# Raw tokens of the next pair in tiles of products 4 and 6, parts made in the order of the products, loads issued by GpSimd

## The chip, the cores and the metric

The kernel runs on one core of one Trainium2 chip. The metric is the device time of one execution in microseconds (us); the figure is the median of the runs. PE is TensorE, DVE is VectorE, ACT is ScalarE, POOL is GpSimd. SP is SyncE, which only issues DMAs here.

## The reference

```python
# q, k, v: (8, 12, 448, 64) f32; w_pre, w_post: (12, 12)
scores = einsum('bhij,hg->bgij', scale * (q @ k^T), w_pre)
attn   = einsum('bhij,hg->bgij', softmax(scores), w_post) @ v
x      = attn as 3584 tokens x 768
h      = x @ w_in                  # 768 x 2048
out    = (h - tanh(h)) @ w_out     # 2048 x 768
```

The change touches only the second half, the feed-forward part from `x` to `out`, and only the way in which its input `x` is brought in.

## The kernel before, in words

The 3584 tokens make seven blocks of 512. Attention runs first, one pipeline of "places" `p` up to `NPL`, and writes `x` to DRAM (`xs`). Block 0 of the feed-forward part is done plainly (`Block0`, 16 steps). The other six blocks are done as three pairs (`s` = 0, 1, 2): a pair's tokens and each weight are split into halves, and the 2x2 matrix product is made with seven products instead of eight (Strassen-Winograd). So each pair needs seven inputs of the first layer, in this order: `b11`, `b21`, `t2`, `t1`, `t3`, `b22`, `t4` (table `WA`). The pair's tokens are four quarters b11, b21, b12, b22 (512 tokens x 384 channels, 768 KB each); three of them are inputs themselves, and the `t` are sums and differences of the four. Each input is held as a high part in fp32r (suffix `h`, a cast on ACT) and a low part (suffix `l`, a subtraction on DVE), since the matmuls are run as three products high x high, high x low, low x high. So there are 14 tiles, one buffer each, and one scratch tile `xr`.

A pair has eight steps (`pair_step`, `p` = 0 to 7). In a step the seven products of one slice of hidden channels run on PE, each 9 matmuls. After product `i`, `between(i)` is called, and then some units of the second layer (`res.units`), 12 matmuls each, which work on results stored earlier: an item of work has two units (four for block 0) and needs one activation tile `gl` (512 KB, loaded by SP, cast to `gh` on ACT, low part on DVE at L449) and a weight tile `w` (768 KB, loaded by SP). The weight tiles of the products are `wa` (384 KB, SP, seven buffers). `gl` and `w` have three buffers each, `gh` two, and they are loaded two items ahead.

Between two pairs lies a transition. PE runs held-back units (18 for s = 0 and s = 1) while DVE and ACT finish the last step (`Late`, v0 to v5) and make the 14 tiles of the next pair. `xq_jobs` is a generator of 11 jobs for that. In the first pair its jobs run within the steps of `Block0`. `xq_loads` is the generator of the loads of the four raw quarters, split by channel third and by sequence, six DMAs a quarter, issued by SP. Raw quarters go to `b11l`, `b21l`, `t3l` and `b22l`. In the last step of a pair (`p` = 7) `between(i)` issues them in small pieces. A load has to wait until the last product that reads its tile is done.

What sets the order: each engine executes its instructions in the order in which the code is written (`in_order` at the end). Each DMA on SP, and likewise each on POOL, signals one of eight semaphores in turn, so an issue waits until the eighth DMA before it on that queue has landed. POOL's own DMAs here are the stores of gate results (`gs<-ga`, `gs<-gb`, `gs<-gs`, from v0 and v5) and of outputs.

Of the kernel before, what the change touches and what calls it, by code (L numbers as in the profile page):

```python
# [21 lines left out]
def raw(ap):  # L22

    return ap.bitcast(F32)
# [126 lines left out]
def kernel_body(  # L151
# [11 lines left out]
    nc = tc.nc  # L163
# [92 lines left out]

    LATER = ("b21h", "b22h", "t4h")

# [300 lines left out]

    def load_xq(name, b, h):  # L560
        x_tiles(name)
        for c in range(HK):
            for to, i, at in runs(b):
                nc.sync.dma_start(raw(ff.xs[name])[:, c, to], xs[i][:, h * HK + c, at])
            yield

    def xq_jobs():

        def sub(x, y):
            nc.vector.tensor_sub(xr, x if x is xr else raw(ff.xs[x]), y if y is xr else raw(ff.xs[y]))  # L570

        def high(x, src):
            x_tiles(x + "h")
            nc.scalar.copy(ff.xs[x + "h"], src)

        def low(x, src):
            nc.vector.tensor_sub(ff.xs[x + "l"], src, raw(ff.xs[x + "h"]))

        def both(x):
            high(x, raw(ff.xs[x + "l"]))  # L580
            low(x, raw(ff.xs[x + "l"]))

        xr = ff.xr.tile([P, HK, TB], F32, name="xr", tag="xr")
        def parts(x):
            high(x, xr)
            low(x, xr)

        sub("t3l", "b11l")
        yield
        x_tiles("t1l")  # L590
        parts("t1")
        yield
        sub("b22l", "t3l")
        yield
        parts("t3")
        yield
        nc.vector.tensor_add(xr, xr, raw(ff.xs["b11l"]))
        yield
        both("b11")
        yield  # L600
        x_tiles("t2l")
        parts("t2")
        yield
        sub("b21l", xr)
        yield
        both("b21")
        yield
        both("b22")
        yield
        x_tiles("t4l")  # L610
        parts("t4")
        yield

    IDLE = ("u", "qa", "qb", "t", "h01", "h23")
    def xq_loads(s):
        ba, bb = 2 * s + 1, 2 * s + 2
        order = (("b11l", ba, 0), ("b21l", ba, 1), ("t3l", bb, 0), ("b22l", bb, 1))
        for x, b, h in order if s else (order[0], order[2], order[3], order[1]):
            yield from load_xq(x, b, h)

# [114 lines left out]
    with ExitStack() as st:  # L735
# [501 lines left out]
        def between0(f):  # L1237
            if f in (10, 12):
                res.more_w2((f - 10) // 2)
            if f in (13, 15):  # L1240
                res.more_gr((f - 13) // 2)
            for _ in range({1: 2, 2: 1, 4: 1, 5: 1, 6: 1, 8: 1, 10: 1, 12: 1, 14: 1}.get(f, 0)):
                next(xq)

        xq, xl = xq_jobs(), xq_loads(0)
        pieces = {NPL - 2: 2, NPL - 1: 3, NPL: 3, NPL + 1: 2, NPL + 2: 2}
        x0 = [partial(parts_x0, c, nc.vector if c < 4 else nc.gpsimd) for c in range(NK)]
# [73 lines left out]
    for s in range(NS):  # L1321
        for p in range(NQ):

            def between(i):
                next(xq, None)
                if p == NQ - 1 and s + 1 < NS:
                    for _ in range((2, 2, 2, 0, 1, 3, 2)[i]):
                        next(xl, None)

# [7 lines left out]
        else:  # L1337
            res.deepen()
        job = partial(next, xq, None)
        jobs = [  # L1340
            [late.v0], [late.v1, late.v2], [late.v3], [late.v4], [late.v5, job], [job, job], [job, job], [job, job], [job, job],
        ]
        n = HELD[s] + AHEAD[s]
        for i in range(0, n, 2):
            res.units(1)
            for f in jobs.pop(0) if jobs else ():
                f()
            for _ in range(2):
                next(xl, None)
            res.units(1)  # L1350
# [37 lines left out]
```

## Time and profile before

| | |
|---|---|
| median of 3 runs | 1745.02 us (1744.99 to 1750.26) |
| profiled execution | 1741.7 us, span of the core 1740.0 us |
| PE busy | 1673.0 us, 96% |
| DVE / ACT / POOL busy | 1232.8 / 1142.9 / 489.3 us |
| block 0 | about 856 to 927 us |
| steps of s = 0 | 927 to 1083 us; transition to about 1132 us |
| steps of s = 1 | to 1330 us; transition to about 1391 us |
| steps of s = 2 and the tail | to 1740 us |

A row of windows gives, for a stretch, its length and then the busy time of each engine, the granted PE clock (1.00 is full), the busy share of the DMA engines and GB/s. In a timeline the first number is the start, the second the duration, and the brackets give idle time ahead of the instruction and what ended it. "DMA" rows in the chain are transfers from issue to landing.

### The profile page before, as it was taken

The numbers are of one execution on the slowest core, as the hardware profiler recorded it, in microseconds if no ns is written. First come the engines' busy times: TensorE is split into PE (matmuls) and PEld (weight loads), VectorE is DVE, ScalarE is ACT, GpSimd is POOL, SyncE is SP. The second block draws the span as 40 slices with busy tenths as digits, with TensorE's granted clock in tenths as the row PEclk, the third lists the DMA queues.
The fourth block names the chain that finished last, engine by engine and source line by source line (L and its number), as shares of the span: only waits on it lengthen the run. The fifth ranks groups of instructions, "written<-read, shape, count | busy, mean of one in ns | idle before, by whom it ended". The sixth has DMA issues, their size and how long they took to land.

```text
span 1740.0 us, 41171 instructions
## 1 busy us (share of the span) xinstructions
PE 1673.0 (96%) x16068; PEld 1391.5 (80%) x16068; DVE 1232.8 (71%) x2119; ACT 1142.9 (66%) x2016; POOL 489.3 (28%) x702
## 2 busy tenths in 40 slices
PE   8999999999999899999998999899998899999999
PEld 6776777777777677777787778788887888889999
DVE  5686777766777777775498899668776768788432
ACT  5777777777778787786486767456665365666331
POOL 1355455555545555551100111101101101101000
PEclk9999999999999999999999999999999899999999
DMA  8778789787887979865778889879989779888993
GB/s 179 212 224 254 229 253 277 234 261 240 244 254 232 260 250 266 260 198 171 234 263 301 283 290 328 321 270 349 317 309 374 286 252 351 297 313 328 406 414 138
DMA packets 322289, 475.09 MB, mean 273 GB/s; under 512 B 105264, under 2 KB 255280, under 8 KB 322096
## 3 DMA queue, kind: packets, MB, share of 16 engines
q1 hardware_dynamic: 305660, 414.34, 73.9%
q0 software_dynamic: 16128, 57.68, 8.6%
q8 instruction: 128, 2.10, 0.5%
q14 instruction: 65, 0.53, 0.1%
q10 hardware_dynamic: 308, 0.43, 0.1%
HBM read 274.73 MB, written 120.59 MB: 227 GB/s over the span
## 4 chain that ended last, share of the span: by engine, by line
PE 76%; DVE 8%; DMA 6%; ACT 6%; issue 3%; SPq 1%; POOL 1%; DVEq 0%; ACTq 0%; POOLq 0%
PE ps_o L956 14%; PE ps_m L998 8%; PE ps_p L917 8%; PE y L533 6%; PE y L531 6%; PE y L532 6%; PE ps_h L290 6%; PE ps_h L291 6%; PE ps_h L293 6%; PE ps_q L873 6%; DMA vr<-in_v_dram 1%; PE ps_m L839 1%; DVE qa L319 1%; DMA t<-s 1%; DMA gl<-gs 1%
## 5 line engine op out<-in xcount | busy, mean ns | idle before, releaser
L956 PEld LDWEIGHTS ps_o<-wr,e 60*112 60x112 f32 (+1 forms) x5760 | 306.1, 175 | 45.2 <-POOL wr L939 12.2
L956 PE MATMUL ps_o<-wr,e 60*112 60x60 f32 (+1 forms) x5760 | 315.4, 259 | 17.2 <-ACT at L966 11.9
L926 DVE TENSOR_REDUCE mx<-ps_p 128x1 f32<-128x448 f32 x360 | 207.3, 618 | 154.3 <-PE ps_p L917 154.0
L928 ACT ACTIVATE e<-ps_p,mx 128x448 f32<-128x448 f32 x360 | 225.7, 634 | 104.2 <-DVE mx L926 93.4
L966 ACT COPY at<-ps_o 112x960 f32<-112x960 f32 x156 | 153.8, 986 | 76.9 <-PE ps_o L956 76.1
L939 POOL TENSOR_TENSOR wr<-wpost,zs 128x120 f32<-128x120 f32 x180 | 69.7, 387 | 422.8 <-DVE zs L938 319.1
L917 PE MATMUL ps_p<-t,wpre 60*64 60x448 f32 (+1 forms) x1440 | 180.9, 570 | 7.0 <-DMA t<-s 5.1
L998 PEld LDWEIGHTS ps_m<-at,vr 112*64 112x64 f32 x3072 | 147.5, 137 | 29.5 <-ACT at L973 11.5
L998 PE MATMUL ps_m<-at,vr 112*64 112x120 f32 (+1 forms) x3072 | 161.8, 261 | 6.8 <-ACT at L973 4.1
L531 PE MATMUL y<-w,gh 128*128 128x384 f32 x448 | 154.1, 344 | 5.7 <-ACT u L306 2.7
L533 PE MATMUL y<-w,gl 128*128 128x384 f32 x424 | 146.6, 346 | 8.1 <-DVE gl L449 8.1
L532 PE MATMUL y<-w,gh 128*128 128x384 f32 x448 | 153.1, 342 | 0.0
L873 PEld LDWEIGHTS ps_q<-kk,qh 64*120 64x120 f32 (+1 forms) x768 | 60.2, 177 | 85.3 <-issue 57.1
L873 PE MATMUL ps_q<-kk,qh 64*120 64x448 f32 (+1 forms) x768 | 124.6, 400 | 2.2 <-DVE kk L825 1.4
L878 DVE COPY s<-ps_q 120x448 f32<-120x448 f32 (+1 forms) x192 | 112.6, 615 | 9.9 <-PE ps_q L873 9.3
L306 ACT ACTIVATE u<-h 128x1024 f32<-128x1024 f32 x56 | 59.5, 1062 | 76.5 <-DVE h L715 71.4
L668 POOL DMA_DIRECT2D gs<-gb x24 | 17.2, 717 | 296.5 <-DVE gb L667 280.8
L878 ACT COPY s<-ps_q 120x448 f32<-120x448 f32 (+1 forms) x192 | 95.4, 539 | 7.0 <-PE ps_q L873 6.7
L443 ACT CAST gh<-gl 128x1024 fp32r<-128x1024 f32 x61 | 63.4, 1039 | 52.6 <-DMA gl<-gs 17.4
L531 PEld LDWEIGHTS y<-w,gh 128*128 128x128 f32 x448 | 86.6, 193 | 10.8 <-ACT u L306 3.0
L533 PEld LDWEIGHTS y<-w,gl 128*128 128x128 f32 x424 | 81.8, 193 | 9.6 <-DVE gl L449 9.5
L532 PEld LDWEIGHTS y<-w,gh 128*128 128x128 f32 x448 | 86.5, 193 | 3.4
(372 smaller groups left out, 3891.2 us busy)
## 6 DMA issues: line engine op xcount, KB each, us to landing
t<-s SPq DMA_DIRECT2D x342, 210.0 KB
wa<-ss SPq DMA_DIRECT2D x96, 384.0 KB
w<-wo SPq DMA_DIRECT2D x43, 768.0 KB
gl<-gs SPq DMA_DIRECT2D x62, 512.0 KB
wa<-wi SPq DMA_DIRECT2D x72, 384.0 KB
w<-ts SPq DMA_DIRECT2D x35, 768.0 KB
gs<-gs POOLq DMA_DIRECT2D x24, 768.0 KB, 9.3
cr<-in_moe_w_in_dram SPq DMA_DIRECT2D x48, 256.0 KB
```

Source lines behind the costliest of these rows:

```text
L290: nc.tensor.matmul(ph, w[:, c, 0], xh, start=start and c == 0, stop=False, skip_group_check=True)
L531: nc.tensor.matmul(y, gh[:, tok], wh, start=first, stop=False, skip_group_check=True)
L532: nc.tensor.matmul(y, gh[:, tok], wl, start=False, stop=False, skip_group_check=True)
L533: nc.tensor.matmul(y, gl[:, tok], wh, start=False, stop=last, skip_group_check=True)
L873: nc.tensor.matmul(ps[:n, :S], qx[a, hp, :], kx[a, hp % 2], start=(x == 0), stop=(x == 2))
L878: eng(sts[i][:n, 2 * hp + j, :], ps[:n, :S])
L917: nc.tensor.matmul(pss[r][halves[j], :], wpre[k, :], ts[j][k, :], start=True, stop=True)
L926: nc.vector.tensor_reduce(out=mx, in_=ps, axis=AX.X, op=ALU.max, negate=True)
L928: nc.scalar.activation(e, ps, AF.Exp, bias=mx, scale=1.0, accum_out=zs[:, 0, r : r + 1])
L956: nc.tensor.matmul(ps[:CP, j, c * GP : (c + 1) * GP].rearrange("p (h i) -> p h i", i=GI)[:, :, r * GH : (r + 1) * GH], e[k, c * CP : (c + ...
L966: nc.scalar.copy(ats[i0][:, :, :, at : at + 2 * GI].rearrange("p c h (j i) -> p j (c h) i", j=2), ps[:CP, :, : NC * GP].rearrange("p j (x ...
L998: nc.tensor.matmul(pv[j * D : (j + 1) * D, r, :n], vt[:, j, c, :], ats[i][:, c, 2 * hp + j, :n], start=(c == 0), stop=(c == NC - 1),)
```

## The change

The raw quarters go into other tiles: b11 into `t1l`, b21 into `b22h`, b12 into `t1h`, and b22 into `b22l`. These belong to products 3 and 5. A quarter is loaded with two DMAs (one per sequence) instead of six. For s = 0 SP issues them; for the two transitions POOL does, three in steps after products 4, 5 and 6, and the fourth after the first held unit. The 11 jobs are reordered to b11, b21, t3, t2, t4, t1, b22; each job keeps its instructions (seven casts on ACT, seven low parts and four sums on DVE). Eight jobs run in block 0 or in a transition and three (the difference for t1, t1's parts, b22's parts) in the next pair's first step, after products 0, 1 and 2; before it was 11 and 0 for the first pair and 9 and 2 for the others.

```diff
-    LATER = ("b21h", "b22h", "t4h")
+    LATER = ("t2h", "t4h", "t4l")
...
-    def load_xq(name, b, h):
+    def load_xq(eng, name, b, h):
         x_tiles(name)
-        for c in range(HK):
-            for to, i, at in runs(b):
-                nc.sync.dma_start(raw(ff.xs[name])[:, c, to], xs[i][:, h * HK + c, at])
-            yield
+        for to, i, at in runs(b):
+            eng.dma_start(raw(ff.xs[name])[:, :, to], xs[i][:, h * HK : (h + 1) * HK, at])
...
     def xq_loads(s):
         ba, bb = 2 * s + 1, 2 * s + 2
-        order = (("b11l", ba, 0), ("b21l", ba, 1), ("t3l", bb, 0), ("b22l", bb, 1))
-        for x, b, h in order if s else (order[0], order[2], order[3], order[1]):
-            yield from load_xq(x, b, h)
+        for x in (("t1l", ba, 0), ("b22h", ba, 1), ("b22l", bb, 1), ("t1h", bb, 0)) if s == 0 else (
+            ("t1l", ba, 0), ("t1h", bb, 0), ("b22h", ba, 1), ("b22l", bb, 1)
+        ):
+            load_xq(nc.gpsimd if s else nc.sync, *x)
+            yield
...
+        parts("b11", at("t1l"), "h", "l")
+        yield
+        parts("b21", at("b22h"), "h", "l")
+        yield
+        xr = fresh()
+        nc.vector.tensor_sub(xr, at("b22l"), at("t1h"))
+        yield
+        parts("t3", xr, "h", "l")
+        yield
+        nc.vector.tensor_add(xr, xr, at("t1l"))
+        yield
+        parts("t2", xr, "h", "l")
+        yield
+        nc.vector.tensor_sub(xr, at("b22h"), xr)
+        yield
+        parts("t4", xr, "h", "l")
+        yield
+        nc.vector.tensor_sub(xr, at("t1h"), at("t1l"))
+        yield
+        parts("t1", xr, "h", "l")
+        yield
+        parts("b22", at("b22l"), "h")
+        yield
...
-            for _ in range({1: 2, 2: 1, 4: 1, 5: 1, 6: 1, 8: 1, 10: 1, 12: 1, 14: 1}.get(f, 0)):
+            for _ in range({1: 1, 2: 1, 4: 1, 6: 1, 8: 1, 10: 1, 12: 1}.get(f, 0)):
                 next(xq)
...
-        pieces = {NPL - 2: 2, NPL - 1: 3, NPL: 3, NPL + 1: 2, NPL + 2: 2}
+        pieces = {NPL - 2: 1, NPL - 1: 1, NPL: 1, NPL + 1: 1}
...
                 next(xq, None)
-                if p == NQ - 1 and s + 1 < NS:
-                    for _ in range((2, 2, 2, 0, 1, 3, 2)[i]):
-                        next(xl, None)
+                if p == NQ - 1 and s + 1 < NS and i >= 4:
+                    next(xl, None)
...
-            [late.v0], [late.v1, late.v2], [late.v3], [late.v4], [late.v5, job], [job, job], [job, job], [job, job], [job, job],
+            [late.v0], [late.v1, late.v2], [late.v3], [late.v4, job], [late.v5, job], [job, job], [job, job], [job, job],
```

The first place is the end of the last step of s = 0. SP's queue there, before: the last of the 24 loads of raw tokens (`xs`), the one weight load of a product among them, and then the activation and weight tiles of the held units.

```order
L564 DMA b22l<-xs_61 128x192
L564 DMA b22l<-xs_62 128x320
L632 DMA wa<-ss_77 128x768
L564 DMA b22l<-xs_61 128x192
L564 DMA b22l<-xs_62 128x320
L564 DMA b22l<-xs_61 128x192
L564 DMA b22l<-xs_62 128x320
L376 DMA gl<-go 128x1024
L375 DMA w_15227<-wo_75 128x1536
L375 DMA w_15264<-wo_75 128x1536
L376 DMA gl<-go 128x1024
```

SP's queue at the same place in the changed kernel:

```order
L624 DMA wa<-ss_77 128x768 x3
L376 DMA gl<-go 128x1024
L375 DMA w_15195<-wo_75 128x1536
L375 DMA w_15235<-wo_75 128x1536
L376 DMA gl<-go 128x1024
L375 DMA w_15269<-wo_76 128x1536
L375 DMA w_15303<-wo_76 128x1536
L403 DMA gl<-gs_90 128x1024
```

All loads of `xs` have left SP's queue, and the tiles of the held units follow the weights of the products directly. POOL's queue in the same stretch, changed kernel (before, it held only the rows `gs` and `out_dram`):

```order
L660 DMA gs_90<-gb 128x2x512
L661 DMA gs_90<-gs 128x3x512
L563 DMA t1l<-xs_60 128x3x256
L563 DMA t1l<-xs_61 128x3x256
L563 DMA t1h<-xs_61 128x3x192
L563 DMA t1h<-xs_62 128x3x320
L563 DMA b22h<-xs_60 128x3x256
L563 DMA b22h<-xs_61 128x3x256
L638 DMA gs_90<-ga 128x2x512
L563 DMA b22l<-xs_61 128x3x192
L563 DMA b22l<-xs_62 128x3x320
```

Eight loads now stand behind the two stores of v5, and the store of v0 stands behind six of them.

The second place is the middle of the transition after s = 1, on DVE: `gl` is the low part for the next item of units, `c` adds results out of PSUM, the rest are jobs. Before:

```order
L570 TENSOR_TENSOR xr<-b22l,t3l 128x1536
L449 TENSOR_TENSOR gl<-gl,gh 128x1024
L577 TENSOR_TENSOR t3l<-xr,t3h 128x1536
L597 TENSOR_TENSOR xr<-xr,b11l 128x1536
L449 TENSOR_TENSOR gl<-gl,gh 128x1024
L550 TENSOR_TENSOR c<-y_17206,c 128x384
L550 TENSOR_TENSOR c<-y_17207,c 128x384
L550 TENSOR_TENSOR c<-y_17208,c 128x384
L550 TENSOR_TENSOR c<-y_17209,c 128x384
L577 TENSOR_TENSOR b11l<-b11l,b11h 128x1536
L577 TENSOR_TENSOR t2l<-xr,t2h 128x1536
L449 TENSOR_TENSOR gl<-gl,gh 128x1024
```

The same items in the changed kernel:

```order
L579 TENSOR_TENSOR t3l<-xr,t3h 128x1536
L449 TENSOR_TENSOR gl<-gl,gh 128x1024
L596 TENSOR_TENSOR xr<-xr,t1l 128x1536
L579 TENSOR_TENSOR t2l<-xr,t2h 128x1536
L449 TENSOR_TENSOR gl<-gl,gh 128x1024
L550 TENSOR_TENSOR c<-y_17162,c 128x384
L550 TENSOR_TENSOR c<-y_17163,c 128x384
L550 TENSOR_TENSOR c<-y_17164,c 128x384
L550 TENSOR_TENSOR c<-y_17165,c 128x384
L600 TENSOR_TENSOR xr<-b22h,xr 128x1536
L579 TENSOR_TENSOR t4l<-xr,t4h 128x1536
L449 TENSOR_TENSOR gl<-gl,gh 128x1024 x2
```

Behind the four `c` stood two low parts; now a difference and the low part made of it stand there, and no job stands between the last two `gl`.

The third place is the first step of s = 0, on DVE: the last gate of block 0 (`ga`), then the sum `h` that takes product 1 out of PSUM. Before:

```order
L326 TENSOR_TENSOR ga<-qa,u 128x1024
L329 COPY_PREDICATED ga<-gs,t 128x1024
L694 TENSOR_TENSOR h_13996<-ps_h,h_13996 128x512
L449 TENSOR_TENSOR gl<-gl,gh 128x1024
L715 TENSOR_TENSOR h_13996<-h_13996,ps_h 128x512
```

In the changed kernel:

```order
L326 TENSOR_TENSOR ga<-qa,u 128x1024
L329 COPY_PREDICATED ga<-gs,t 128x1024
L604 TENSOR_TENSOR xr<-t1h,t1l 128x1536
L686 TENSOR_TENSOR h_13975<-ps_h,h_13975 128x512
L579 TENSOR_TENSOR t1l<-xr,t1h 128x1536
L579 TENSOR_TENSOR b22l<-b22l,b22h 128x1536
L449 TENSOR_TENSOR gl<-gl,gh 128x1024
L707 TENSOR_TENSOR h_13975<-h_13975,ps_h 128x512
```

Three jobs have come in around `h`, and three fewer stand in block 0 ahead of these rows.

More of the change, by code (lines that the diff above doesn't have):

```diff
@@ L558, in x_tiles, with xq_loads @@
             ff.xs[x] = x_tile_of(x)
-    def load_xq(name, b, h):
+    def load_xq(eng, name, b, h):
         x_tiles(name)
-        for c in range(HK):
-            for to, i, at in runs(b):
-                nc.sync.dma_start(raw(ff.xs[name])[:, c, to], xs[i][:, h * HK + c, at])
+        for to, i, at in runs(b):
+            eng.dma_start(raw(ff.xs[name])[:, :, to], xs[i][:, h * HK : (h + 1) * HK, at])
+    def xq_loads(s):
+        ba, bb = 2 * s + 1, 2 * s + 2
+        for x in (("t1l", ba, 0), ("b22h", ba, 1), ("b22l", bb, 1), ("t1h", bb, 0)) if s == 0 else (
+            ("t1l", ba, 0), ("t1h", bb, 0), ("b22h", ba, 1), ("b22l", bb, 1)
+        ):
+            load_xq(nc.gpsimd if s else nc.sync, *x)
@@ L565, in load_xq @@
             yield
     def xq_jobs():
[L569 to L588, printed above, removed]
+        def parts(x, src, *tiles):
+            x_tiles(*[x + t for t in tiles])
+            hi, lo = ff.xs[x + "h"], ff.xs[x + "l"]
+            nc.scalar.copy(hi, src)
+            nc.vector.tensor_sub(lo, src, raw(hi))
+        def fresh():
+            return ff.xr.tile([P, HK, TB], F32, name="xr", tag="xr")
+        def at(x):
+            return raw(ff.xs[x])
+        parts("b11", at("t1l"), "h", "l")
@@ L589, in xq_jobs @@
         yield
-        x_tiles("t1l")
-        parts("t1")
+        parts("b21", at("b22h"), "h", "l")
         yield
-        sub("b22l", "t3l")
+        xr = fresh()
+        nc.vector.tensor_sub(xr, at("b22l"), at("t1h"))
         yield
-        parts("t3")
+        parts("t3", xr, "h", "l")
         yield
-        nc.vector.tensor_add(xr, xr, raw(ff.xs["b11l"]))
+        nc.vector.tensor_add(xr, xr, at("t1l"))
         yield
-        both("b11")
+        parts("t2", xr, "h", "l")
         yield
-        x_tiles("t2l")
@@ L602, in xq_jobs @@
-        parts("t2")
+        nc.vector.tensor_sub(xr, at("b22h"), xr)
         yield
-        sub("b21l", xr)
+        parts("t4", xr, "h", "l")
         yield
-        both("b21")
+        nc.vector.tensor_sub(xr, at("t1h"), at("t1l"))
         yield
-        both("b22")
+        parts("t1", xr, "h", "l")
         yield
-        x_tiles("t4l")
-        parts("t4")
+        parts("b22", at("b22l"), "h")
         yield
     IDLE = ("u", "qa", "qb", "t", "h01", "h23")
-    def xq_loads(s):
-        ba, bb = 2 * s + 1, 2 * s + 2
-        order = (("b11l", ba, 0), ("b21l", ba, 1), ("t3l", bb, 0), ("b22l", bb, 1))
-        for x, b, h in order if s else (order[0], order[2], order[3], order[1]):
-            yield from load_xq(x, b, h)
@@ L1347, in kernel_body @@
                 f()
-            for _ in range(2):
-                next(xl, None)
+            next(xl, None)
             res.units(1)
```

## The prediction

> **What bounds the kernel now.** The page says that PE is busy for nearly the whole span, so only stretches where PE stands still, or runs at a lower granted clock, can give time back.
>
> ```profile
> span 1740.0 us, 41171 instructions
> PE 1673.0 (96%) x16068; PEld 1391.5 (80%) x16068; DVE 1232.8 (71%) x2119; ACT 1142.9 (66%) x2016; POOL 489.3 (28%) x702
> ```
>
> Windows over the places that the change touches come next: the gates of block 0, its end with the first step of s = 0, the transition after s = 0, then the last step of s = 1 and the two halves of the transition behind it.
>
> ```profile
> 882.00:926.00 44.00, 44.00 (x195) 36.44 (x195) 42.23 (x34) 40.54 (x43) 3.25 (x6) 1.00 0.84 290
> 926.00:945.00 19.00, 14.42 (x63) 10.68 (x62) 15.79 (x14) 12.46 (x15) 1.21 (x3) 1.00 0.95 344
> 1083.00:1107.00 24.00, 18.68 (x98) 16.11 (x97) 17.89 (x16) 9.90 (x11) 2.18 (x3) 0.93 0.93 352
> 1300.00:1326.00 26.00, 26.00 (x129) 23.14 (x128) 20.06 (x19) 16.69 (x21) 1.80 (x3) 1.00 1.00 363
> 1326.00:1360.00 34.00, 28.37 (x133) 26.86 (x131) 21.94 (x22) 14.73 (x17) 6.56 (x11) 0.85 0.89 333
> 1360.00:1395.00 35.00, 28.85 (x139) 27.07 (x138) 24.31 (x21) 14.08 (x13) 3.63 (x6) 0.90 0.78 286
> ```
>
> In block 0 PE never waits (44.00 of 44.00), though DVE is 96% busy. PE then stands for 4.6 us up to 945. The first transition costs 5.3 us of idle time and 7% of clock, the second 5.6 + 6.2 us and 15% and 10% of clock. There are about 25 us to be had in all.
>
> Who PE waits for, in the first transition and then in the second:
>
> ```profile
> PE y L501 <- DMA w<-wo: 5.3, 1, 5.3
> PE y L531 <- ACT c L509: 1.4, 1, 1.4
> ...
> PE y L533 <- DVE gl L449: 8.1, 4, 2.8
> PE y L531 <- ACT u L306: 2.7, 1, 2.7
> PE y L531 <- DMA w<-ts: 1.0, 1, 1.0
> ```
>
> The chain of the first transition runs through the raw loads, and SP's own waits name why: its issues of raw tokens (L564) waited for PE to give a tile free and for earlier transfers to land.
>
> ```profile
> 1071.38 5.76 DMA b21l<-xs
> 1077.16 6.33 DMA w<-wo
> 1083.51 7.60 DMA t3l<-xs
> 1091.19 0.34 SPq L376
> 1091.57 7.00 DMA w<-wo
> 1098.70 0.77 PE y L501
> ...
> SPq L564 <- PE ps_h L291: 3.1, 1, 3.1
> SPq L564 <- DMA t3l<-xs: 2.2, 2, 1.6
> ...
> 1084.82 0.40 PE L501 MATMUL y<-w,gh 128*128 128x512 f32 x1
> ```
>
> So the weight tile that PE wanted at 1093.4 (5.3 ahead of 1098.7) was issued at 1091.57, since the small loads stood ahead of it. The last row is the first held unit: it starts a new item, which sets free the buffers for that issue, so the issue was some 6 us late.
>
> **The change, part by part.**
>
> *Raw loads off SP, first transition.* SP then issues `gl` and `w` at about 1085. A landing of 7.00 us as in the chain ends at 1092.3, ahead of 1093.4. The 5.3 us of waiting go, and with them the lowered clock behind it: 7% of 18.68 is 1.3. The wait on `c L509` (1.4) came from two casts that ACT ran between two groups of copies; now one cast stands there, so I take it as gone too. Against that, POOL's four quarters now move in the same 20 us in which the units load. Three weight tiles fall in that time, each with a lead of 8.3 us against landings of 7.0 to 9.1 (the last from a row below), so 0 to 0.8 late each: 0 to 2.4, and I take 1.5. Sum: -5.3 - 1.3 - 1.4 + 1.5 = -6.5.
>
> *The same in the second transition, first half.* The rows of two starts of items on PE, of SP's queue, of the cast and the matmul that waited, and the GB/s over 1326 to 1360 in 40 slices:
>
> ```profile
> 1326.25 0.33 PE L531 MATMUL y<-w,gh 128*128 128x384 f32 x1
> ...
> 1332.54 0.33 PE L531 MATMUL y<-w,gh 128*128 128x384 f32 x1
> ...
> 1327.98 0.81 SPq L403 DMA_DIRECT2D gl<-gs  x1
> ...
> 1332.10 4.04 SPq L564 DMA_DIRECT2D b22l<-xs  x4
> 1336.24 0.48 SPq L403 DMA_DIRECT2D gl<-gs  x1
> 1337.48 0.32 SPq L393 DMA_DIRECT2D w<-ts  x1
> 1337.55 1.04 ACT L443 CAST gh<-gl 128x1024 fp32r<-128x1024 f32 x1 [5.27 <-DMA gl<-gs]
> 1346.55 0.41 PE L531 MATMUL y<-w,gh 128*128 128x384 f32 x1 [1.00 <-DMA w<-ts]
> ...
> GB/s 410 347 396 395 381 370 357 323 355 396 424 433 420 409 281 267 409 401 396 425 448 412 405 414 417 400 416 406 399 336 101 0 0 0 81 207 207 316 372 401
> ```
>
> Items start on PE at 1326.3, 1332.5 and, without stalls, at 1336.7 and 1340.9; each start releases the buffers for the item two further on. The second pair of loads (1336.24 and 1337.48) was due at 1332.5, so SP was 4 to 5 us late with it. The landings took 9.5 us (1327.98 to 1337.5) and 9.1 (1337.48 to 1346.5). Issued on time and landing alike, the first pair arrives at 1336 (no stall) and the second at 1342.1, 1.2 after its item. Of this half's loss of 5.6 idle and 15% of 28.37 (4.3), together 9.9, that would leave 1.2.
>
> But the transfers themselves move later. Before, one quarter (0.79 MB) and, as I estimate, half of another were still to come at 1326. Now all four are, since on POOL they stand behind the stores of v5:
>
> ```profile
> 1326.78 0.75 POOL L669 DMA_DIRECT2D gs<-gs  x1
> ```
>
> That is 3.15 - 1.18 = 1.97 MB more in a stretch where the engines run full (28 slices, mean 390 GB/s): 5.0 us, if nothing of it finds a gap. The ends: 0 (the three empty slices, 2.6 us, and the thin ones behind them take it) and 6.1 (all of 2.36 MB). I take 5.0, since the DMA engines were at 1.00 already in 1300 to 1326 and SP's queue can't load further ahead than its buffers. So 9.9 becomes 6.2: -3.7.
>
> A rule speaks against this size. The Trainium skill, page "DMA: Bandwidth & Descriptors", section "SWDGE vs HWDGE vs iDMA", says that each DMA engine takes turns between the queue that GpSimd feeds and those that hardware feeds. By it SP's tiles would get half the rate as long as GpSimd's transfers last, and the sum would be that of the slower rival below, which is worked out there from rows; no row here has so long an overlap of the two queues.
>
> *Jobs in the second half.* Rows on ACT and DVE of the jobs between two `gl`:
>
> ```profile
> 1364.28 1.05 ACT L443 CAST gh<-gl 128x1024 fp32r<-128x1024 f32 x1 [3.11 <-DMA gl<-gs]
> 1365.24 1.47 ACT L574 CAST t1h<-xr 128x1536 fp32r<-128x1536 f32 x1
> ...
> 1366.74 1.76 DVE L577 TENSOR_TENSOR t1l<-xr,t1h 128x1536 fp32r<-128x1536 f32 x1 [2.60 <-ACT t1h L574]
> 1368.54 1.76 DVE L570 TENSOR_TENSOR xr<-b22l,t3l 128x1536 f32<-128x1536 f32 x1
> 1370.21 1.22 DVE L449 TENSOR_TENSOR gl<-gl,gh 128x1024 fp32r<-128x1024 f32 x1
> ...
> 1378.81 1.94 DVE L550 TENSOR_TENSOR c<-y,c 128x384 f32<-128x384 f32 x4
> ```
>
> `gh` starts, a cast (1.47) and two DVE operations (1.7 each) follow, then `gl` (1.2): 7.1 us, while an item lasts 4.2. That is why PE waits for `gl`. With the new order the sum comes before the cast and doesn't wait for it, so two of these chains shrink by 1.7 us. The third grows: behind the four `c` (1.9) come a difference (1.7), a cast that waits for it (1.5), its low part (1.8) and `gl`, 8.1 us, where 1.9 + 1.7 + 1.7 + 1.2 = 6.5 stood. The last chain sets when this half ends, so what the first two give the third takes back: 0, with -3.4 (both kept) and +1.6 as ends.
>
> *Three jobs moved to the next step.* In block 0 they took no time from PE (44.00 of 44.00), so only its end counts:
>
> ```profile
> 939.00 1.36 DVE L329 COPY_PREDICATED ga<-gs,t 128x1024 f32<-128x1024 int32 x1
> 940.22 0.71 DVE L694 TENSOR_TENSOR h<-ps_h,h 128x512 f32<-128x512 f32 x1
> ```
>
> Product 3 started behind that `h`, at 941.0. Two of the jobs that leave stood in the gate chain, 1.75 each, so the last gate ends 3.5 us earlier, at 936.7. Then t1's three pieces come in, and product 3 reads them: 1.7 + 1.5 + 1.8 in a row, with a little to hand over, until 941.7. So the gain is eaten: +0.6 (ends -1.1, if `h` alone counts, and +2). In the first step of s = 1, b22's parts stand ahead of a `gl`: the chain behind product 2 is 0.7 (an evacuation like that of `h`) + 1.5 + 1.8 + 1.2 = 5.2, and the matmul that needs it comes a unit, a product and two matmuls later, 2.1 + 2.1 + 0.4 = 4.6, so +0.6. In s = 2 no item begins there: 0.
>
> *At nothing.* The loads for block 0 (8 instead of 24 on SP, the same bytes): PE has no wait on them, and the reader of the last quarter comes in step 2; with that cover gone, a late quarter would hold DVE ahead of the gates. The waits that POOL gets: v0's store stands behind six loads there, and nobody reads it within the transition.
>
> **Sum:** -6.5 - 3.7 + 0 + 0.6 + 0.6 = -9.0 us. The profiled execution took 1741.7 us (1.7 of it around the span), which would be 1732.7. It lies 3.3 below the median of 1745.0, so the median goes to 1736.0.
>
> **The rivals.** *Transfers collide as before* (0.21). SP is free sooner, but the bytes meet on the same engines, the second transition gives 0, and half of the 5.3 stays in the first: -6.5 + 2.7 + 1.2 = -2.6, 1742.4. For it: DMA at 0.93 to 1.00 in all these rows. Against it: the empty slices around 1351, in which PE ran slow and SP had nothing free to issue. The Trainium skill, same page, section "Issuing engines are not separate DMA queues", holds that issuing from several engines saves only the issuing time; by that the time would be near this rival's. The rows agree that SP's time was the one on the chain.
>
> *Slower* (0.12): SP's tiles get only half of the rate. POOL moves 5.8 MB from 1326 on (three stores of 0.52, 0.79 and 0.52, outputs 0.79, quarters 3.15); at 195 GB/s that lasts 30 us. An item's 1.31 MB then take 6.7 us instead of 4.2, so the 4.4 items in that time lose 11.0, with the clock's 4.3 as now 15.3 in place of 9.9: +5.4. The first transition's item (2.1 MB) takes 10.8 instead of 8.4, three times: 7.2 in place of 8.0, -0.8. With the steps' +1.2 the sum is +5.8: 1750.8. It decides where `gl` takes over 10.5 us to land in 1326 to 1350.
>
> *More* (0.14): the second half also clears, as `gl` lands in 4.4 us. Its 6.2 idle and 10% of 28.85 go: -9 further, 1727.0.
>
> *The change doesn't do what it says*: `gl` and `w` are held by the wait for PE that the `wa` ahead of them has, not by the raw loads. Then -1, inside the first rival's chance, since the chain shows t3l.
>
> **How the numbers follow.** A change of 0.3% (5.2 us) is about what these runs can tell from none. Likeliest case 0.53, with its own bounds -14 to -5: nearly all of it, and the 0.14, are faster: 0.66. The first rival and the rest of the likeliest case are the same: 0.23. The slower one reaches over 0.3% in most of its chance: 0.11. The range takes in "more" up to 1726 and the slower case up to 1747.
>
> **What would show it.** Right: no wait of PE on `w` over 2 us in the first transition; `gl` issued by SP within 1 us of the item's start; the waits on `gl` in the second half still there, the longest behind the four `c`; product 3 of the first step waiting for t1's parts. Wrong: DMA landings of over 10 us, or a cast of b11 or b21 that waits for its quarter with `gh` behind it.

## The result and the profile after

The changed kernel takes 1755.9 us in the median of 20 runs, the kernel before 1745.5 us on the same chip: the ratio is 1.0064 (95% interval 1.0044 to 1.0084), so it is slower by 10 to 11 us, where 9 us less were predicted. The profiled execution of the changed kernel has a span of 1753.1 us, against 1740.0. The first page lines of the changed kernel, and its windows over the same stretches as before (the gates of block 0, their end with the first step of s = 0, the first transition, the second one in two halves):

```profile
span 1753.1 us, 41121 instructions
PE 1676.5 (96%) x16068; PEld 1391.8 (79%) x16068; DVE 1232.1 (70%) x2119; ACT 1143.1 (65%) x2016; POOL 501.6 (29%) x718
```

```profile
882.00:926.00 44.00, 44.00 (x196) 36.42 (x194) 41.13 (x32) 36.48 (x41) 3.33 (x6) 1.00 0.86 291
926.00:950.00 24.00, 16.70 (x61) 12.18 (x60) 20.14 (x16) 16.07 (x17) 1.14 (x3) 0.86 0.76 283
1089.00:1113.00 24.00, 17.89 (x89) 15.38 (x88) 18.29 (x16) 11.74 (x12) 8.61 (x12) 0.86 1.01 369
1337.00:1371.00 34.00, 26.79 (x135) 25.12 (x134) 24.84 (x24) 16.17 (x18) 11.31 (x18) 0.93 1.01 382
1371.00:1406.00 35.00, 26.90 (x132) 25.07 (x132) 21.24 (x17) 11.69 (x11) 3.65 (x6) 0.92 0.74 272
```

PE does the same work, in 3.5 us more of busy time (1676.5 us against 1673.0), which is the lower clock; the other 10 of the 13 us are standing time. In the first transition and in the first half of the second the DMA engines are now at 1.01, and PE is busy for less of each of these windows than before.

Where the time went is read best from the PE timeline. The stretches between the same matmuls hold the same work in both kernels; for instance, the first matmul of `b11` in a step. Of the changed kernel (start of the first two steps of s = 0):

```profile
928.26 0.43 PE L290 MATMUL ps_h<-b11h,wa 128*128 128x512 f32 x1
...
962.04 0.40 PE L290 MATMUL ps_h<-b11h,wa 128*128 128x512 f32 x1
```

Such differences, in us, for both kernels (a transition runs from the last matmul of a pair's last step to the first of the next pair):

| stretch | before | after | difference | predicted |
|---|---|---|---|---|
| up to block 0 (attention, not changed) | 855.5 | 857.2 | +1.7 | 0 |
| block 0 | 71.8 | 71.0 | -0.8 | 0 |
| first step of s = 0 | 28.2 | 33.8 | +5.6 | +0.6 |
| other steps of s = 0 | 127.2 | 127.2 | 0.0 | 0 |
| first transition | 48.9 | 52.8 | +3.9 | -6.5 |
| first step of s = 1 | 27.2 | 27.9 | +0.7 | +0.6 |
| other steps of s = 1 | 171.6 | 171.6 | 0.0 | 0 |
| second transition | 60.3 | 61.5 | +1.2 | -3.7 |
| s = 2 and the tail | 349.2 | 350.1 | +0.9 | 0 |

The first step of s = 0 and the two transitions carry it. The waits of PE in them, in the order first step, first transition, second transition:

```profile
PE ps_h L290 <- ACT t1h L578: 3.7, 1, 3.7
PE ps_h L291 <- DVE t1l L579: 1.0, 1, 1.0
...
PE y L501 <- DMA w<-wo: 6.1, 1, 6.1
PE y L531 <- ACT c L509: 2.4, 1, 2.4
...
PE y L533 <- DVE gl L449: 9.0, 5, 3.5
PE y L531 <- DMA w<-wo: 3.9, 1, 3.9
PE y L531 <- DMA w<-ts: 1.7, 1, 1.7
```

The waits that the change was expected to remove in the first transition (5.3 on `w`, 1.4 on `c`) are still there, each a little longer. So is the idle time of the second one's first half, which was expected to go nearly whole: 7.2 us against 5.6, now on weight tiles (3.9 and 1.7) more than on `gl`. The waits on t1's parts are new.

The first transition. The chain of waits of the changed kernel, and then the share of the two DMA queues in 1092 to 1106 (packets, MB, share of the 16 engines):

```profile
1091.50 0.32 SPq L376
1091.87 13.97 DMA w<-wo
1105.97 0.77 PE y L501
```

```profile
q0 software_dynamic: 773, 2.86, 63.4%
q1 hardware_dynamic: 400, 1.99, 36.4%
```

SP issued `gl` and `w` within a microsecond of the item's start, as predicted. But `w` needed 13.97 us to land, in place of 7.00, in a stretch in which POOL's queue (q0), with all four quarters in it, held 63.4% of the engines' time. In the kernel before, the same queue had 29.9% of a like stretch (1084 to 1099), and SP's 73.2%:

```profile
q1 hardware_dynamic: 2190, 4.20, 73.2%
q0 software_dynamic: 496, 1.84, 29.9%
```

The quarters were also missing ahead of the transition. In the last 5 us of the step the DMA engines of the changed kernel were at 0.64 and 200 GB/s, since the loads stood on POOL's queue behind the stores of v5; in the kernel before they were at 1.02 and 371 GB/s. The difference, 0.86 MB, is about one quarter. The changed kernel comes first:

```profile
1084.40:1089.40 5.00, 5.00 (x23) 4.14 (x23) 4.54 (x7) 2.99 (x3) 1.43 (x2) 1.00 0.64 200
1077.90:1082.90 5.00, 5.00 (x24) 4.14 (x23) 4.54 (x7) 2.96 (x3) 1.40 (x2) 1.00 1.02 371
```

The first step of s = 0, on DVE, ACT and PE, changed kernel:

```profile
939.29 1.38 DVE L329 COPY_PREDICATED ga<-gs,t 128x1024 f32<-128x1024 int32 x1
940.54 1.76 DVE L604 TENSOR_TENSOR xr<-t1h,t1l 128x1536 f32<-128x1536 f32 x1
...
942.34 1.47 ACT L578 CAST t1h<-xr 128x1536 fp32r<-128x1536 f32 x1 [4.60 <-DVE xr L604]
...
943.84 1.76 DVE L579 TENSOR_TENSOR t1l<-xr,t1h 128x1536 fp32r<-128x1536 f32 x1 [0.94 <-ACT t1h L578]
...
943.86 0.80 PE L290 MATMUL ps_h<-t1h,wa 128*128 128x512 f32 x1 [3.73 <-ACT t1h L578]
945.65 0.80 PE L291 MATMUL ps_h<-t1l,wa 128*128 128x512 f32 x1 [1.00 <-DVE t1l L579]
```

The last gate's last operation starts at 939.29, 11.0 us into the step; it started at 939.00 before, 11.6 us in, so it came only 0.6 us sooner, though two jobs have gone from the queue ahead of it. Behind it t1's three pieces run one after another, and product 3 reads them at once. It starts 15.6 us into the step, where it started 13.6 us in before. Then PE is slow as well; the row of windows for the 5 us behind the wait shows a granted clock of 0.50:

```profile
945.00:950.00 5.00, 4.34 (x10) 3.47 (x11) 3.49 (x3) 2.14 (x3) 0.00 (x0) 0.50 0.02 9
```

### The profile page after: what moved, and what is told of

It is laid out like the page before. It is cut to its first block, busy times and chain, and to the rows that moved or that the text cites. A ratio compares the mean times of both kernels' runs of the same rounds, so it can differ in the third digit from the quotient of the medians.

```text
span 1753.1 us, 41121 instructions
## 1 busy us (share of the span) xinstructions
PE 1676.5 (96%) x16068; PEld 1391.8 (79%) x16068; DVE 1232.1 (70%) x2119; ACT 1143.1 (65%) x2016; POOL 501.6 (29%) x718
## 4 chain that ended last, share of the span: by engine, by line
PE 76%; DMA 7%; DVE 7%; ACT 6%; issue 3%; SPq 0%; POOL 0%; DVEq 0%; ACTq 0%; POOLq 0%
PE ps_o L948 13%; PE ps_m L990 8%; PE ps_p L909 8%; PE ps_h L291 7%; PE ps_h L290 7%; PE ps_h L293 7%; PE ps_q L865 6%; PE y L531 6%; PE y L533 6%; PE y L532 6%; DMA t<-s 2%; PE ps_m L831 1%; ACT e L920 1%; ACT at L958 1%; DMA w<-wo 1%
## 5 line engine op out<-in xcount | busy, mean ns | idle before, releaser
L865 PEld LDWEIGHTS ps_q<-kk,qh 64*120 64x120 f32 (+1 forms) x768 | 61.1, 179 | 86.7 <-issue 61.5
L443 ACT CAST gh<-gl 128x1024 fp32r<-128x1024 f32 x61 | 63.4, 1039 | 36.4 <-DMA gl<-gs 19.0
```

Source lines behind the costliest of these rows:

```text
L865: nc.tensor.matmul(ps[:n, :S], qx[a, hp, :], kx[a, hp % 2], start=(x == 0), stop=(x == 2))
```

## The experiments

The theories: the loss in the transitions comes from POOL's queue taking rate from SP's tiles (1), or from the new order of the jobs (2), or from the tiles wanted last, which come free last, so that all four quarters load in the transition (3). For the first step there is one theory, t1's chain, with its opposite that block 0 has no room for the jobs. The medians are of 10 to 12 runs (20 for the changed kernel and the kernel before); the intervals are of the ratio to the kernel before on the same chip (e1 to e4 ran on one chip, e5 to e13 on another, so across these two groups the ratios compare better than the medians). The runs of one program spread over 8 to 24 us, and the attention, whose code is the same in all, took from 855.5 to 868.4 us in the profiled executions. So I read effects of a few us from the stretches of the profile and use the medians as the check.

| kernel | median (us) | ratio (95%) | first step s = 0 | transition 1 | transition 2 |
|---|---|---|---|---|---|
| before | 1745.5 | | 28.2 | 48.9 | 60.3 |
| changed | 1755.9 | 1.0064 (1.0044 to 1.0084) | 33.8 | 52.8 | 61.5 |
| e1: changed, quarters on SP | 1756.6 | 1.0069 (1.0048 to 1.0089) | 33.4 | 49.7 | 61.2 |
| e2: changed, jobs in block 0 | 1750.6 | 1.0041 (1.0022 to 1.0061) | 28.9 | 52.9 | 61.7 |
| e3: e1 and e2 | 1750.7 | 1.0044 (1.0023 to 1.0065) | 28.8 | 50.5 | 60.4 |
| e4: before, whole quarters on POOL | 1741.6 | 0.9972 (0.9954 to 0.9990) | 27.5 | 48.3 | 53.5 |
| e5: e4, loads as late as changed | 1746.6 | 0.9999 (0.9980 to 1.0017) | 28.4 | 50.5 | 61.5 |
| e7: e2, two quarters not loaded | 1745.3 | 1.0001 (0.9982 to 1.0020) | 28.8 | 51.3 | 55.8 |
| e8: e4, third quarter early | 1743.1 | 0.9991 (0.9968 to 1.0013) | 28.4 | 46.6 | 53.5 |
| e9: before, whole quarters on SP | 1743.1 | 0.9986 (0.9967 to 1.0005) | 28.2 | 47.8 | 56.5 |
| e10: e2, casts freed | 1742.5 | 0.9969 (0.9943 to 0.9994) | 28.9 | 49.2 | 58.7 |
| e11: e7 and e10 | 1740.1 | 0.9976 (0.9957 to 0.9995) | 28.9 | 49.0 | 52.3 |
| e12: e8, on SP | 1744.6 | 1.0000 (0.9983 to 1.0016) | 28.0 | 48.5 | 57.3 |
| e13: e8 again | 1741.3 | 0.9973 (0.9955 to 0.9991) | 28.6 | 46.6 | 57.7 |

### e1: the queue

```diff
-            load_xq(nc.gpsimd if s else nc.sync, *x)
+            load_xq(nc.sync, *x)
```

> The changed kernel with one edit: SP issues the whole quarters of s >= 1 too, GpSimd none of them. Theory 1 (GpSimd's queue takes more than half of the DMA rate from the tiles that SP loads): in the first transition w lands in about 7 us again, where it took 13.97, and the two transitions give back 3.8 + 1.1 us, so about 5 us less than the changed kernel, 1751 us by the medians. The wait in front of product 3 of the first step stays (3.7 us). Rival (the new order of the jobs makes the transitions slow, the queue does not): the transitions stay as they are, 1756 us. Second rival (SP's wait for tiles is back and costs as much): w is issued 5 us late, and the time is again 1755 us.

The median did not move (1756.6). In the profile, the first transition gave back 3.1 us and the second 0.3. `w` landed in 11.61 us in place of 13.97, so the issuer has a part in the first transition, though not nearly the whole of the landing:

```profile
1094.77 11.61 DMA w<-wo
```

So the issuer matters where the quarters load late (3.1 of 3.9 us in the first transition), but with SP as issuer both transitions are no shorter than before, and the expected 5 us did not come. Nor is it shown that the queue's share made the 3.1 us. SP doesn't stand behind the stores of v5, so the four quarters left 4 to 8 us earlier. Of the first one, e1 and then the changed kernel (their first transitions start at 1092.3 and 1089.4):

```profile
1084.50 1.00 SPq L563 DMA_DIRECT2D t1l<-xs  x2
```

```profile
1089.43 1.50 POOL L563 DMA_DIRECT2D t1l<-xs  x2
```

Theory 1 is at most a part, not the cause of the whole.

### e2 and e3: the first step

```diff
-            for _ in range({1: 1, 2: 1, 4: 1, 6: 1, 8: 1, 10: 1, 12: 1}.get(f, 0)):
+            for _ in range({1: 2, 2: 1, 4: 1, 5: 1, 6: 1, 8: 1, 10: 1, 12: 1, 14: 1}.get(f, 0)):
```

> The changed kernel with one edit: block 0 makes all eleven jobs, by the table of the kernel before, so that none is left for the first step of s = 0. Theory 2 (t1's chain of difference, cast and low part behind the last gate delays product 3): the first step is as long as before, so 5 us less than the changed kernel, about 1751 us, and no wait of product 3 on t1's parts. Rival (block 0's gates end no earlier with fewer jobs because DVE is full, so putting the jobs back lengthens the gates): the time stays at 1755 us or grows by 2 to 3 us.

5.3 us less by the medians (ratio 1.0041 after 1.0064), 4.9 by the first step, and block 0 no longer (70.6 us against 71.0). In the waits of PE around the first step t1's parts are gone; what is left are waits like those of the kernel before, which were 1.0 on `gh` and 1.1 on the same `h`:

```profile
PE ps_h L290 <- ACT gh L443: 1.6, 1, 1.6
PE ps_h L290 <- DVE h L686: 1.4, 1, 1.4
```

So the three jobs in the first step cost 5 us, and in block 0 they cost nothing.

> Both edits: quarters on SP, and all jobs in block 0. Theories 1 and 2 together, if they add: 1756 - 5 - 5 = 1746 us, the time of the kernel before within 2 us. If the new order of the jobs has a cost of its own in the transitions, 1750 us or more; if it has a gain once the queue is right, under 1743 us.

1750.7 us, the value named for a cost of the new order in the transitions. Its stretches come to 1.1 us more than those of before behind the attention; the median says 6.5. I count on no more than that it is not faster than the kernel before.

### e4: the queue and the whole quarters, without the rest

```diff
-                nc.sync.dma_start(raw(ff.xs[name])[:, c, to], xs[i][:, h * HK + c, at])
+                if c == 0:
+                    nc.gpsimd.dma_start(raw(ff.xs[name])[:, :, to], xs[i][:, h * HK : (h + 1) * HK, at])
```

(for s >= 1; block 0's loads, the tiles and the jobs stay as they were)

> The kernel before with one edit: the quarters of s >= 1 are loaded whole by GpSimd, at the place of each quarter's first piece; tiles, jobs and block 0 as before. Theory 1: the first transition loses about 4 us and the second 1, so 1750 us; w lands in over 10 us. Rival (the job order is what costs): 1745 us as before, or less, since SP issues on time; my prediction's mechanism would give 1736 to 1740 us here.

This is faster than the kernel before, 0.9972 (0.9954 to 0.9990), though 1741.6 us is a little above the range of 1736 to 1740 that my mechanism gave. By the profile nearly all of it is the second transition, 53.5 us against 60.3 (how well such a figure repeats is seen at e13). There the waits on `gl` fall from 8.1 to 5.9:

```profile
PE y L533 <- DVE gl L449: 5.9, 4, 2.6
```

In the first transition it gains only 0.6 us, for a reason that its SP queue and the chain show:

```profile
1094.01 0.32 SPq L376
...
1094.38 12.54 DMA w<-wo
```

`w` was issued at once, some 6 us earlier than before with respect to the item, and it landed 5.5 us more slowly (12.54 against 7.00): 15.0 us into the transition, where it had landed 15.7 us in. The late issue had only hidden that the transfers themselves were the limit. POOL's queue held 64.6% of the engines' time here too (1094.4 to 1107), so that share alone doesn't tell the changed kernel from this one. The Trainium skill, page "DMA: Bandwidth & Descriptors", section "Issuing engines are not separate DMA queues", says that another issuing engine saves only the time of issuing, since all run on the same DMA engines. The first transition agrees with it (0.6 us); in the second one 6.8 us came with the quarters off SP's queue and in fewer pieces, and e9 will show about half of that without another issuer.

### e5, e7 and e8: when the quarters load

e5 moves e4's loads to the places that they have in the changed kernel:

```diff
-                if p == NQ - 1 and s + 1 < NS:
-                    for _ in range((2, 2, 2, 0, 1, 3, 2)[i]):
-                        next(xl, None)
+                if p == NQ - 1 and s + 1 < NS and i >= 4:
+                    next(xl, None)
```

> The kernel before with whole quarters of s >= 1 loaded by GpSimd, and these loads moved to the places that they have in the changed kernel: behind products 4, 5 and 6 of the last step and into the transition; tiles and jobs are those of the kernel before. The stretch from the end of the last step to the first product of the next pair took 48.9 us in the first transition and 60.3 in the second in the kernel before, 52.8 and 61.5 in the changed one, 48.3 and 53.5 where GpSimd alone is the edit. Theory (late bytes: a tile wanted last is free last, so all four quarters run in the transition against the tiles of the items): 52 to 53 and 60 to 62 us, so about 1751 us. Rival (the chains of difference, cast and low part in the new order of jobs cost the time): 48.3 and 53.5 us as with early loads, 1741 us.

The first transition took 50.5 us (+2.2 against e4), the second 61.5 (+8.0), as long as in the changed kernel. The ratio went from 0.9972 to 0.9999, so all that e4 had gained was lost (the median is 1746.6, where about 1751 was expected). Late loads alone make the second transition as long as the changed kernel's; of the first they make about half (50.5 where 52 to 53 was expected). The loads on POOL's queue, e4 first and e5 below it, show what was moved:

```profile
1318.84 1.51 POOL L567 DMA_DIRECT2D b11l<-xs  x2
1320.33 1.49 POOL L567 DMA_DIRECT2D b21l<-xs  x2
1334.51 1.50 POOL L567 DMA_DIRECT2D t3l<-xs  x2
```

```profile
1327.71 1.50 POOL L567 DMA_DIRECT2D b11l<-xs  x2
1329.20 2.21 POOL L518 DMA_DIRECT2D out_dram<-c  x4
1336.41 0.75 POOL L567 DMA_DIRECT2D b21l<-xs  x1 [5.01 <-DMA gs<-gb]
```

In e4 two quarters leave 14 us ahead of the last step's stores (`gs`), which are issued at 1333.0 to 1334.5; in e5, and in the changed kernel, all four stand behind them, where the eight DMAs that may be under way on POOL's queue also hold them up. The changed kernel can't load as early as e4: its tiles belong to products 3 and 5.

e7 goes the other way, from e2:

```diff
-            load_xq(nc.gpsimd if s else nc.sync, *x)
+            if s == 0 or x[0] in ("t1l", "t1h"):
+                load_xq(nc.gpsimd if s else nc.sync, *x)
...
-            return raw(ff.xs[x])
+            return raw(ff.xs[x if s == 0 else {"b22h": "t1l", "b22l": "t1h"}.get(x, x)])
```

> The changed kernel with all jobs in block 0, and two of the four quarters (ba's and bb's second halves) of s >= 1 not loaded: the jobs read the other two in their place, so the output of the later pairs isn't the reference's; instructions on DVE and ACT are the same. With all four its two transitions took 52.9 and 61.7 us. Theory (late bytes): 1.57 MB less in each transition, so 48 to 49 and 53 to 54 us, like the kernel whose first two quarters load early; about 1738 us. Rival (the order of the jobs): both stay within 1 us, 1750 us.

-1.6 us in the first transition and -5.9 in the second: bytes are most of the second and a small part of the first. PE's wait on `w` in the first transition hardly moved (5.6 us, 6.0 in e2): the quarters left out are the two that are issued last. The ratio fell from e2's 1.0041 to 1.0001. The expectation of 48 to 49 for the first transition failed, so something else is in it.

e8 brings a third quarter ahead of the transition:

```diff
-        order = (("b11l", ba, 0), ("b21l", ba, 1), ("t3l", bb, 0), ("b22l", bb, 1))
+        order = (("b11l", ba, 0), ("b21l", ba, 1), ("t2l", bb, 0), ("b22l", bb, 1))
...
-                    for _ in range((2, 2, 2, 0, 1, 3, 2)[i]):
+                    for _ in range((2, 2, 3, 0, 0, 3, 2)[i]):
```

(t3 then gets its own new tile, t2's low part stays where the raw quarter was)

> The kernel before with whole quarters of s >= 1 by GpSimd, and bb's first half kept raw in t2l instead of t3l, which is free two products earlier, and loaded right behind product 2, ahead of the last stores of gates: three quarters then load ahead of the transition and one in it. Theory (late bytes): the second transition falls further, from 53.5 to about 50 us (8.0 us were lost for two quarters more, so 4 each), the first from 48.3 to about 46; 1736 us. Rival (bytes are not what is left there; gl waits on the jobs): no change beyond 1 us, 1741 us.

The first transition fell by 1.7 us, as expected, the second not at all. In the run repeated as e13 the second took 57.7 us, so one profile of a second transition is good to about 4 us; the first repeats to the tenth (46.6 both times).

### e9: fewer loads, still on SP

```diff
-        for c in range(HK):
-            for to, i, at in runs(b):
-                nc.sync.dma_start(raw(ff.xs[name])[:, c, to], xs[i][:, h * HK + c, at])
+        for to, i, at in runs(b):
+            nc.sync.dma_start(raw(ff.xs[name])[:, :, to], xs[i][:, h * HK : (h + 1) * HK, at])
```

(at the place of each quarter's first piece, s >= 1)

> The kernel before with whole quarters of s >= 1, two loads each in place of six, still issued by SP, at the place of each quarter's first piece. If the number of loads in SP's queue is what counted: near the time with GpSimd, 48.3 and 53.5 us in the transitions, 1741 us. If SP's waits for tiles and earlier landings count: 48.9 and 60.3 us as before, 1745 us.

47.8 and 56.5 us, 0.9986 (0.9967 to 1.0005): between the two expectations. In the first transition SP issued `w` at 1094.38, 2.5 us in, just as in e4 (8.7 us in before), though the quarters were on its own queue. So it was the many pieces, spread between the products, that had made the issue late there, and a part of e4's gain, perhaps half, needs no other engine, only whole quarters issued early.

### e10 and e11: the order of the jobs

In the new order each difference stands in DVE's queue right ahead of the cast that reads it, so ACT waits for DVE. ACT's rows of the changed kernel in the first transition:

```profile
1132.20 0.40 ACT L511 COPY c<-y 128x256 f32<-128x256 f32 x1
1134.85 1.47 ACT L578 CAST t4h<-xr 128x1536 fp32r<-128x1536 f32 x1 [2.24 <-DVE xr L600]
1136.22 0.47 ACT L508 COPY c<-y 128x384 f32<-128x384 f32 x1
```

PE waits for that `c`. e10 (from e2) frees these casts:

```diff
-            nc.scalar.copy(hi, src)
+            nc.scalar.copy(hi, src if s == 0 or x in ("b11", "b21", "b22", "t1") else at("t1l"))
```

> The changed kernel with all jobs in block 0; for s >= 1 the casts of t3, t2 and t4 read the raw tile of ba's first half instead of the difference that DVE makes in the job ahead (their output isn't the reference's; instructions and sizes are the same). ACT then doesn't wait for DVE's difference. Theory (serial chains): the wait of the held unit on c in the first transition goes from 2.4 back to 1.4 us or less, the first transition from 52.9 to 51 or 52 us, the second from 61.7 to about 60. Rival (all is late bytes): 52.9 and 61.7 us within 0.5.

(The expectation says that the output isn't the reference's. In fact the low part is still the difference less the high part, so the two together still make the difference, and the output stays close to the reference's; how exact it is was not measured.) ACT goes straight on, and the wait on `c` is gone from the first transition:

```profile
1138.78 0.40 ACT L511 COPY c<-y 128x256 f32<-128x256 f32 x1
1139.04 1.51 ACT L578 CAST t4h<-t1l 128x1536 fp32r<-128x1536 f32 x1
1140.42 0.51 ACT L508 COPY c<-y 128x384 f32<-128x384 f32 x1
```

The first transition fell by 3.7 us and the second by 3.0; the wait on `gl` there went from 9.0 to 5.8. More than the 2.4 us of waiting came back in the first transition, since the clock did too. The windows around the place, e2 and then e10:

```profile
1123.00:1137.00 14.00, 11.56 (x57) 10.28 (x56) 9.98 (x7) 7.28 (x15) 4.30 (x8) 0.88 0.93 301
```

```profile
1134.00:1147.00 13.00, 12.90 (x70) 11.09 (x70) 9.22 (x6) 5.84 (x15) 4.32 (x8) 1.00 0.91 296
```

The ratio fell from e2's 1.0041 to 0.9969. So waiting for the difference costs the changed kernel 3.7 us in the first transition. In the second the 3.0 us are less than two profiles of one kernel can differ by (4 us, see e8 and e13).

> The same casts freed, and two of the four quarters not loaded as well (output of the later pairs isn't the reference's). With two quarters out alone the transitions took 51.3 and 55.8 us; the kernel before with quarters loaded by GpSimd, two of them early, took 48.3 and 53.5. Theory (bytes and serial chains together are the whole of the loss): 49 to 50 and 53 to 54 us. Rival (something else in the order of the jobs, such as b11's and b21's parts a place sooner in ACT's and DVE's queues): no change against 51.3 and 55.8.

49.0 and 52.3 us: at the values that bytes and chains together gave for the first transition, and below them for the second. With both taken out the transitions are as short as e4's, within 1.2 us, so in the first one no third cause of that size is left; in the second one, none above the 4 us by which single profiles differ. Against e7 the freed casts are worth 2.3 and 3.5 us here, the same way as in e10.

What the new order costs against the old one is read from e5 and e2. Both load at the same places and on POOL's queue; they differ in the tiles and in the order of the jobs. From e5 to e2 the first transition grows by 2.4 us (50.5 to 52.9) and the second by 0.2 (61.5 to 61.7). e10's 3.7 is more than that, because it also takes away the 1.4 us that PE waited for `c` in the old order.

### e12 and e13: towards the best version

e12 is e8 with SP as the issuer, with `nc.sync` in place of `nc.gpsimd`.

> The kernel before with whole quarters, bb's first half in t2l and loaded behind product 2, all issued by SP. With GpSimd as issuer the transitions took 46.6 and 53.5 us. If GpSimd's queue as such takes rate from SP's tiles, the first transition falls further, to 44 to 46 us; if SP's waits for tiles come back in another place, the steps ahead of the transitions or the second transition grow by 2 to 4 us. Time 1740 to 1744 us.

The first transition grew by 1.9 us where it was expected to fall: here SP is the worse issuer. With late tiles (e1) it was the better one by 3.1. So POOL's queue is not bad as such: its worth depends on what else stands on it.

> The kernel with three quarters loaded early by GpSimd (bb's first half in t2l), once more unchanged, as the candidate for the best version: its transitions again 46.6 and 53.5 us within 1 us, and its time under that of the kernel before by 3 to 8 us.

0.9973 (0.9955 to 0.9991), 3.9 us under the kernel before on the same chip. In this version and in e4 the quarters load early on POOL, with the tiles and jobs of before (but for t2l in place of t3l here), and in these runs both beat both kernels. The same version run as e8 could not be told from the kernel before (0.9991, 0.9968 to 1.0013), and between it and e4 the runs decide nothing. The expected 53.5 us of the second transition did not repeat (57.7).

## Why the prediction was wrong

*What held.* SP issued `gl` and `w` on time. The waits on `gl` in the second half stayed, the longest (3.5) at its end, behind the four `c`. The first step of s = 1 grew by 0.7 (+0.6 predicted), and block 0's loads cost nothing. And the core of the change, whole quarters off SP's queue, is a gain of some 7 us in the two transitions (e4: 0.6 and 6.8), though a smaller one than the 6.5 and, before counting bytes, 8.7 (9.9 less 1.2) that I had. (The "about 25 us to be had in all" are the two transitions; with the 4.6 us of the first step the rows add up to 30.)

*First step: +0.6 predicted, +5.6 measured.* The step that failed is "so the last gate ends 3.5 us earlier". DVE is 96% busy in 882 to 926, but the last gates don't wait for its queue: they follow ACT, and ACT follows PE, as a row of each in the changed kernel shows, and DVE's freed time turned into such idle time.

```profile
924.38 0.59 ACT L353 COPY h<-ps_h 128x512 f32<-128x512 f32 x1 [1.91 <-PE ps_h L293]
...
927.15 1.23 DVE L315 SCALAR_TENSOR_TENSOR qa<-qa,h 128x1024 f32<-128x1024 f32 x1 [1.90 <-ACT qa L307]
```

So t1's 5 us chain came on top of the gate instead of in its place. Of the 5.6 us, 2.0 are the later start of product 3 and 1.0 its second wait; the rest is the lowered clock behind them (PE is busy for 2.6 us more in this step than before), which I had not counted there.

*First transition: -6.5 predicted, +3.9 measured.* The step that failed is "A landing of 7.00 us as in the chain ends at 1092.3". That landing was of a tile that SP issued only when three quarters had landed; of the fourth some 0.4 MB still moved beside it. Issued on time it met more: 12.54 us in e4, with 1.6 MB of quarters beside it, and 13.97 with all four quarters late. It landed 15.7 us into the transition before, 15.0 in e4 and 16.5 in the changed kernel. So the 5.3 us of waiting were bytes, not SP's issue, as the rival "Transfers collide as before" had it (its first transition, -3.8, was still too good), and the sign "DMA landings of over 10 us" was there. The 0 to 2.4 us for later landings was sized by the very landings (7.0 to 9.1) that had to change. Second, "I take it as gone too" of the wait on `c`: it grew to 2.4, because the one cast that stands there now waits for DVE's difference. I had read from the order that one cast replaces two, and not asked what the one waits for. The way from the kernel before to the changed one goes over e4, e5 and e2: -0.6 for whole quarters on POOL, +2.2 for loading them late, +2.4 for the new tiles and order of the jobs, -0.1 for moving three jobs out of block 0, in all +3.9.

*Second transition: -3.7 predicted, +1.2 measured.* By the same way it is -6.8, +8.0, +0.2 and -0.2. The mechanism was seen and mis-sized: the gain was put at 8.7 and came out as 6.8, and the term of bytes moved into the transition was 5.0, where e4 against e5 gives 8.0 (e2 against e7, with two quarters not loaded at all, 5.9). "Jobs in the second half", taken at 0, held (+0.2). Two chains did shrink: from one `gl` to the next DVE took 6.1 us twice, where it had taken 7.3 and 7.5. The third took what was forecast, 8.0 us from the four `c` to the end of the first `gl` (forecast 8.1), as two rows of the changed kernel show:

```profile
1389.62 1.94 DVE L550 TENSOR_TENSOR c<-y,c 128x384 f32<-128x384 f32 x4
...
1396.44 2.36 DVE L449 TENSOR_TENSOR gl<-gl,gh 128x1024 fp32r<-128x1024 f32 x2
```

The sizes of the two large terms are good to no more than 4 us, as e8 and e13 differ by that much, and from e4 to e5 the ratio moved by 0.27%, some 5 us, where the stretches of the two transitions say 10.2. That the transition did not get shorter by 3.7 us is better founded: e2, whose transition is the same, repeats the changed kernel's 61.5 us within 0.2, and of the 10 to 11 us by which the medians differ the first transition and the two first steps make 10.2. The kernel before has one profile only.

*The rival "Slower"* had the right sign and nearly the right queue (POOL's at more than half), but put the loss in the second transition, where the measured one is smallest. POOL's queue had the larger share in 1092 to 1106, though in e4 as well. The Trainium skill's rule there (page "DMA: Bandwidth & Descriptors", section "SWDGE vs HWDGE vs iDMA") was that each DMA engine takes turns between the queues; the measured shares, 63.4% and 36.4%, are not halves, and whether SP's queue had work all the time is not shown. By e1 the issuer is worth 3.1 us of the first transition and 0.3 of the second, with quarters that also left earlier.

*Left open.* How much of e4's gain is SP's freed queue and how much the whole quarters: e9 says about half each, but single profiles of the second transition differ by 4 us. A second scratch tile, which might free the new order's chain without changing what the casts read, was not tried. And a busy share is not a rate: in 1092.0 to 1096.4 the changed kernel's DMA engines were at 0.97 but moved 262 GB/s, where e4's moved 400 GB/s at 1.03 in the like stretch (1094.5 to 1098.9). Why, no run here shows.

## What to carry to other kernels

Before an issue is moved earlier, look at the DMA share behind it: at 0.93 to 1.00, as here, the tile landed when the bytes around it were through, and what helped was moving other bytes out of the stretch. Where raw data is parked in a tile that is read last, it can only be loaded last; park it in the tile that comes free first, and look at what stands ahead of the load on its queue (here stores, while the DMA engines stood at 0.64). A job that is moved next to its consumer needs its whole chain counted (difference, cast, low part, and the wait of each engine for the other), plus the lowered clock behind a wait of a few us on PE.

## What the runs showed of the hardware

A weight tile of 768 KB landed in 7.00 us when issued late, behind most of the quarters' transfers, and in 12.54 and 13.97 us when issued some 6 us earlier into the transition, with the DMA engines at 1.0 in all three cases. Behind waits of 3.7 and 6.1 us in the changed kernel PE's granted clock was about half over the next 5 us (0.50 in 945 to 950, and 0.55 in the row below). Behind the 5.3 us wait of the kernel before it was 0.50 for 2.5 us and 0.83 for the next 2.5. So such a wait costs more than its own length.

```profile
1106.00:1111.00 5.00, 5.00 (x16) 4.24 (x17) 4.44 (x5) 0.14 (x1) 0.19 (x1) 0.55 1.03 410
```
